# q and k of an attention kernel turned by VectorE in 32x32 blocks instead of by TensorE through PSUM

## Chip, cores and metric

The kernel runs on one core of a Trainium2 chip. The metric is the device time of one execution in microseconds (us). The core's engines are TensorE (PE; its weight loads are listed as PEld), VectorE (DVE), ScalarE (ACT), GpSimd (POOL) and SyncE (SP), which here only issues DMA transfers. Each engine works through its own instructions in order, and they wait for one another by semaphores.

## The reference, cut to what matters

An attention block whose scores are masked by a hash of q and k, followed by a Fourier mixing block with an MLP. Batch 4, 8 heads, 768 tokens, head dimension 64; everything is float32.

```python
q_bits = (einsum('bhsd,dk->bhsk', q, proj) > 0)          # 6 bits; the same for k
q_bucket = sum(q_bits * 2 ** arange(6), axis=-1)          # the same for k
mask = q_bucket[:, :, :, None] == k_bucket[:, :, None, :]
scores = where(mask, q @ k.T / sqrt(64), -1e9)
attn = softmax(scores)
x = (attn @ v), heads side by side                        # (4, 768, 512)

u = x + real(fft(fft(x, axis=1), axis=2))
un = layernorm(u)
out = u + relu(un @ w_ch1) @ w_ch2                        # 512 -> 2048 -> 512
```

## The kernel before

Two heads are handled together as a **pair**: 4 batches of 4 pairs, n = 0 to 15. The channels of both heads (2 x 64) fill the 128 partitions, so the scores need q and k with channels on partitions and tokens along the free dimension (`qt`, `kt`, 128 x 768), while DRAM holds tokens by rows of 64 channels. One tile with tokens on partitions is loaded per tensor:

```python
def load(n, names="qkv", second=nc.sync):
    b, t = divmod(n, NPAIR)
    for nm in names:
        src = {"q": q, "k": k, "v": v}[nm]
        tag, bufs = ("vn", 2) if nm == "v" else ("qkn", 2)
        tl = wt([P, NT, 2, D], F32, tag, f"{nm}n{n}", bufs)      # P=128, NT=6, D=64
        for h in range(2):
            (second if h else nc.sync).dma_start(
                tl[:, :, h, :], src[b, 2 * t + h].rearrange("(p c) d -> p c d", c=NT)
            )
        nat[nm, n] = tl
```

q and k share two buffers of the tag `qkn`: the q tile of a pair takes the buffer of the q tile of the pair before it, and k that of k.

`prepare(n)` turns the tiles by TensorE: six transposes of 128x128 for q and six for k, three in one PSUM bank, each bank copied to SBUF by VectorE or ScalarE in turn (`evac`). In the pairs of `LITE` after pair 0 all these copies go to ScalarE. Then come the sums of squares for a later check (`norm`) and the hash bits.

```python
def evac(dst, src, act=False):
    flip[0] ^= 1
    if flip[0] and not act:
        nc.vector.tensor_copy(dst, src)
    else:
        nc.scalar.copy(dst, src)

def prepare(n):
    lite = n in LITE                      # LITE = (0, 1, 2, 3, 4)
    act = lite and n > 0
    ts = {}
    for io, nm in enumerate("qk"):
        tn = nat.pop((nm, n))
        tt = wt([P, S], F32, nm + "t", f"{nm}t{n}")
        for g in range(2):
            ps = pt([P, 3, P], f"tr{nm}{n}_{g}")
            for i in range(3):
                c = 2 * i + g if nm == "q" else 3 * g + i
                nc.tensor.transpose(
                    ps[:, i, :], tn[:, c].rearrange("p h d -> p (h d)"), ident
                )
            if nm == "q":
                for i in range(2):
                    dst = tt[:, i * HALF + g * HALF // 2 : i * HALF + (g + 1) * HALF // 2]
                    evac(
                        dst.rearrange("p (j c) -> p c j", c=3),
                        ps[:, :, i * D : (i + 1) * D], act,
                    )
            else:
                evac(tt[:, g * HALF : (g + 1) * HALF],
                     ps.rearrange("p c t -> p (c t)"), act)
        ts[nm] = tt
        yield
        norm(n, io, tn)                   # ScalarE: squares of tn, summed by partition
    ...                                   # hash bits of q and k, from ts
```

q's tokens are stored with even tokens ahead of odd ones within each half, as the Fourier part needs them; k's order is free as long as v has the same.

The scores, their exponentials and the product with v run in six steps a pair; the next pair is prepared beside them, from the second step on:

```python
def attention(b):
    for t in range(NPAIR):
        n = NPAIR * b + t
        if 1 < n + 1 < NPAIR * B:
            load(n + 1)
        ahead = prepare(n + 1) if n + 1 < NPAIR * B else iter(())
        ...
        for c in range(NT):
            new = weigh(n, c)             # score products, Exp (ACT, L834), mask
            ...                           # sums of the weights (DVE, L913)
            while pending:
                finish()                  # product with v (L851)
            ...
            if c > 0:
                next(ahead, None)
            yield
```

PSUM has eight banks: two double banks `sc` for scores, two banks `o` for the product with v, and two banks `ps` for all the rest (`pt`), which are the transposes, the hash bits and every product of the MLP. The attention of batch 0 runs beside the conversion of the MLP's first weights, in the order of the program. The attention of batches 1 to 3 runs beside the Fourier part and the MLP of the batch before, in an order that the compiler's scheduler chose. The MLP uses fast (seven-product) matrix multiplication; its weight combinations are kept in DRAM and fetched by SyncE into a ring of twelve tiles (`w<-ad`), and into larger tiles (`w<-bd`).

At the end the largest norms of q and k decide whether a second, general kernel has to run in place of this one; for these inputs it doesn't:

```python
nc.vector.tensor_tensor(mt[:, 3:4], mt[:, 0:1], mt[:, 1:2], op=ALU.mult)
nc.vector.tensor_scalar(mt[:, 4:5], mt[:, 3:4], (SAFE / SCALE) ** 2, None, op0=ALU.is_gt)
```

Of the kernel before, what the change touches and what calls it, by code (L numbers as in the profile page):

```python
# [11 lines left out]
F32 = mybir.dt.float32  # L12
# [4 lines left out]
AF = mybir.ActivationFunctionType  # L17
ALU = mybir.AluOpType
AX = mybir.AxisListType

P = 128
B, H, S, D = 4, 8, 768, 64
# [3 lines left out]
NT = S // P  # L26
# [9 lines left out]
SCALE = 1.0 / float(np.sqrt(D))  # L36
# [7 lines left out]
SAFE = 36.0  # L44
# [435 lines left out]
def _main(  # L480
# [13 lines left out]
    nc = tc.nc  # L494
# [13 lines left out]
    def wt(shape, dtype, tag, name, bufs=2):  # L508
        return work.tile(shape, dtype, tag=tag, name=name, bufs=bufs)
# [12 lines left out]

    flip = [0]

    def evac(dst, src, act=False):

        flip[0] ^= 1
        if flip[0] and not act:
            nc.vector.tensor_copy(dst, src)
        else:  # L530
            nc.scalar.copy(dst, src)  # L531


    nat = {}

    def load(n, names="qkv", second=nc.sync):
        b, t = divmod(n, NPAIR)
        for nm in names:
            src = {"q": q, "k": k, "v": v}[nm]
            tag, bufs = ("vn", 2) if nm == "v" else ("qkn", 2)  # L540
            tl = wt([P, NT, 2, D], F32, tag, f"{nm}n{n}", bufs)
            for h in range(2):
                (second if h else nc.sync).dma_start(
                    tl[:, :, h, :], src[b, 2 * t + h].rearrange("(p c) d -> p c d", c=NT)
                )
            nat[nm, n] = tl

    load(0, "qk", nc.scalar)
    warm = const.tile([1, 1], F32, tag="warm", name="warm")
# [153 lines left out]
    def norm(n, io, tn):  # L703
        junk = wt([P, S], BF16, "junk", f"sq{io}_{n}", 1)
        nc.scalar.activation(
            junk, tn.rearrange("p c h d -> p (c h d)"), AF.Square,
            accum_out=norms[:, io, n : n + 1],
        )

    def prepare(n):  # L710

        lite = n in LITE
        act = lite and n > 0
        ts = {}
        for io, nm in enumerate("qk"):
            tn = nat.pop((nm, n))
            tt = wt([P, S], F32, nm + "t", f"{nm}t{n}")
            for g in range(2):  # L720
                ps = pt([P, 3, P], f"tr{nm}{n}_{g}")
                for i in range(3):
                    c = 2 * i + g if nm == "q" else 3 * g + i
                    nc.tensor.transpose(
                        ps[:, i, :], tn[:, c].rearrange("p h d -> p (h d)"), ident
                    )
                if nm == "q":
                    for i in range(2):
                        dst = tt[:, i * HALF + g * HALF // 2 : i * HALF + (g + 1) * HALF // 2]
                        evac(  # L730
                            dst.rearrange("p (j c) -> p c j", c=3),
                            ps[:, :, i * D : (i + 1) * D], act,
                        )
                else:
                    evac(
                        tt[:, g * HALF : (g + 1) * HALF],
                        ps.rearrange("p c t -> p (c t)"), act,
                    )
            ts[nm] = tt
            yield  # L740
            norm(n, io, tn)
        if lite:


            qk = wt([P, 2, S], BF16, "qb", f"qkb{n}")
            for io, nm in enumerate("qk"):
                for g in range(2):
                    cols = slice(g * HALF, (g + 1) * HALF)
                    ps = pt([P, HALF], f"bits{nm}{n}_{g}")
                    nc.tensor.matmul(ps, pjw, ts[nm][:, cols], start=True, stop=True)  # L750
                    bits = qk[:, io, cols]
                    nc.vector.tensor_scalar(
                        bits, ps, 0.0, off[:, io : io + 1],
                        op0=ALU.is_gt, op1=ALU.subtract,
                    )
                    if io == 0:
                        nc.vector.tensor_scalar(bits, bits, BIG, None, op0=ALU.mult)
                yield
            preps[n] = ts["q"], ts["k"], qk, None
            return  # L760

        ps = pt([P, HALF], f"bits{n}")
        for j in range(4):
            src = ts["qk"[j // 2]][:, (j % 2) * HALF : (j % 2 + 1) * HALF]
            nc.tensor.matmul(
                ps[32 * j : 32 * j + 32, :], pj, src, start=True, stop=True
            )
        bt = wt([P, HALF], BF16, "bt", f"bt{n}")
        nc.vector.tensor_scalar(bt, ps, 0.0, None, op0=ALU.is_gt)
        yield  # L770

        qb = wt([P, 2, S], BF16, "qb", f"qb{n}")
        kb = wt([P, 2, NT], F32, "kb", f"kb{n}")
        for h in range(2):
            ps = ps_sc.tile([P, 2, 512], F32, tag="sc", name=f"qb{n}_{h}")
            for g in range(2):
                rows = slice(32 * g, 32 * g + 32)
                with behind() if g + h else nullcontext():
                    last[0] = nc.tensor.matmul(
                        ps[:, g, 0:HALF], pw[rows, h, :], bt[rows, :],  # L780
                        start=True, stop=True,
                    )
            evac(qb[:, h, :].rearrange("p (g s) -> p g s", g=2), ps[:, :, 0:HALF])
        ps = ps_sc.tile([P, 2, 512], F32, tag="sc", name=f"kb{n}")
        for c in range(NT):
            g, i = divmod(c, NT // 2)
            rows = slice(64 + 32 * g, 96 + 32 * g)
            with behind() if c else nullcontext():
                last[0] = nc.tensor.matmul(
                    ps[:, g, 2 * i : 2 * i + 2], bt[rows, i * P : (i + 1) * P],  # L790
                    pw[rows, :, 0], start=True, stop=True,
                )
        nc.vector.tensor_copy(
            kb.rearrange("p h (g i) -> p g i h", g=2),
            ps[:, :, 0:NT].rearrange("p g (i h) -> p g i h", h=2),
        )
        preps[n] = ts["q"], ts["k"], qb, kb
# [48 lines left out]
    def values(n, c, pk, oos):  # L846

        for g in range(2):
            w = HALF + 1 - g
            for h in range(2):  # L850
                nc.tensor.matmul(  # L851
                    oos[g][h * D : (h + 1) * D, 0:w], nat["v", n][:, c, h, :],
                    pk[:, g, h, 0:w], start=(c == 0), stop=(c == NT - 1),
                )

# [229 lines left out]
    at = NR * 2 * P  # L1085
# [326 lines left out]
    for b in range(B):  # L1412
        if b > 0:

            wait = 0
            if b == 1:
                next(other)
                next(other)  # L1420
                wait = 2
            steps, done = NPAIR * NT - wait, 2 if b == 1 else 0
            for i, _ in enumerate(attention(b), 1):
                if b == 1 and i == 2:
                    for f, avg in means:
                        centre(f, avg)
                while done * steps < (MIX[b - 1] - LEFT) * (i - wait):
                    next(other)
                    done += 1
        if b == B - 1:  # L1430
            roomy[0] = True


            ms = const.tile([P, 3], F32, tag="ms", name="ms")
            nc.vector.tensor_reduce(ms[:, 0:2], norms, axis=AX.X, op=ALU.max)
            nc.vector.tensor_reduce(ms[:, 2:3], strange, axis=AX.X, op=ALU.max)
            ps = pt([1, 3, P], "norms_t")
            for io in range(3):
                nc.tensor.transpose(ps[:, io, :], ms[:, io : io + 1], ident)
            mt = const.tile([1, 5], F32, tag="mt", name="mt")  # L1440
            nc.vector.tensor_reduce(mt[:, 0:3], ps, axis=AX.X, op=ALU.max)
            nc.vector.tensor_tensor(mt[:, 3:4], mt[:, 0:1], mt[:, 1:2], op=ALU.mult)
            nc.vector.tensor_scalar(
                mt[:, 4:5], mt[:, 3:4], (SAFE / SCALE) ** 2, None, op0=ALU.is_gt
            )
            fl = const.tile([1, 1], I32, tag="fl", name="fl")
            nc.vector.scalar_tensor_tensor(
                fl, mt[:, 2:3], 0.0, mt[:, 4:5], op0=ALU.is_gt, op1=ALU.max
            )
            large = nc.values_load(fl[0:1, 0:1], min_val=0, max_val=1)  # L1450
        for _ in other:
            pass
        other = mix(b)
        if b == 0:
            arrival2 = weights2()
            other = after(2 + NT, other, islice(arrival2, HF + 1))
# [47 lines left out]
```

## Time and profile before

The median of three executions is 1155.78 us (1155.18 to 1157.42). The profiled execution has a span of 1153.1 us.

| what | where it is read | value |
|---|---|---|
| granted TensorE clock, mean | list of cores | 0.995 |
| instructions | head of the page | 14159 |
| DMA packets | slices | 126414, of which 81408 under 512 B |
| bytes moved | slices | 103.13 MB, mean 89 GB/s |
| load of one q or k tile | DMA issues | two transfers of 192 KB, 3.4 and 3.5 us to landing |
| ring load `w<-ad` | DMA issues | 128 KB, 2.0 us to landing, 168 of them |
| one exponential `pk<-sc` (L834) | groups | 808 ns on ACT, 192 of them |

A line of a group names the source line, the engine, the operation, the tile written and those read, and the shape; behind the count come the busy time of the group in us and the mean of one in ns, and then the idle time of the engine just ahead of these instructions, with what ended it. L529 and L531 are the two copies inside `evac`, so they stand for all its callers; the tile names tell them apart. L724 is the transpose. Busy times of matmuls overlap, as TensorE pipelines them, and idle time of an engine that bounds nothing costs nothing.

### The profile page before, as it was taken

The page shows a single profiled execution, that of the slowest core. Times are in us where ns is not written, and L with a number is a line of the kernel's source. Part 1 is how long each engine was busy: PE and PEld are TensorE (multiplying, and loading weights), DVE is VectorE, ACT ScalarE, POOL GpSimd, SP SyncE. Part 2 cuts the span into 40 slices and gives each one's busy share as a digit, 9 for nine tenths or more (in the row PEclk, how much of TensorE's full clock was granted, in tenths as well). Part 3 has the DMA queues.
Part 4 walks back from the last instruction along what each step waited for, and adds up shares of the span by engine and source line. Part 5 has one row for each costly group of instructions (what it writes and reads, how often), then busy time and mean ns, then how long its engine had stood idle before and what let it go on. Part 6 is the DMA issues. An engine that isn't in the chain of part 4 may idle for free. (4 is left out here: it accounts for less than half of the span.)

```text
span 1153.1 us, 14159 instructions
## 1 busy us (share of the span) xinstructions
PE 1092.3 (95%) x5065; PEld 669.3 (58%) x5065; DVE 803.5 (70%) x1445; ACT 464.8 (40%) x892; POOL 81.3 (7%) x157
## 2 busy tenths in 40 slices
PE   7989888899998999999999999999999999999996
PEld 4444344454754576644674467654575468768675
DVE  4889968728689487884867777885775877644352
ACT  6778345524155223345224531345424431341420
POOL 1000000002100011020000002002000002000002
PEclk9999999999999999999999999999999999999998
DMA  9524144600126115013042315013114214131401
GB/s 271 153 79 122 39 138 141 217 16 19 28 83 228 51 51 192 14 51 105 19 151 65 88 51 179 14 42 96 46 34 135 65 31 170 43 92 61 142 19 39
DMA packets 126414, 103.13 MB, mean 89 GB/s; under 512 B 81408, under 2 KB 113280, under 8 KB 126336
## 3 DMA queue, kind: packets, MB, share of 16 engines
q1 hardware_dynamic: 118608, 82.35, 24.3%
q0 software_dynamic: 6160, 19.40, 5.2%
q8 instruction: 42, 0.69, 0.2%
q10 hardware_dynamic: 1568, 0.39, 0.2%
q14 instruction: 36, 0.29, 0.1%
HBM read 81.14 MB, written 20.97 MB: 89 GB/s over the span
## 5 line engine op out<-in xcount | busy, mean ns | idle before, releaser
L1188 PE MATMUL o<-w,h 128*128 128x256 f32 x1152 | 259.5, 381 | 0.3
L1188 PEld LDWEIGHTS o<-w,h 128*128 128x128 f32 x1152 | 216.1, 190 | 41.0 <-issue 4.9
L834 ACT ACTIVATE pk<-sc 128x768 f32<-128x768 f32 x192 | 147.9, 808 | 89.9 <-PE sc L830 63.7
L840 DVE SCALAR_TENSOR_TENSOR pk<-qb,kb,pk 128x768 f32<-128x768 bf16 x132 | 129.5, 1013 | 53.7 <-ACT pk L834 53.6
L851 PE MATMUL oo<-pk,vn 128*64 128x385 f32 (+1 forms) x768 | 149.8, 498 | 5.1 <-ACT x L863 3.6
L830 PE MATMUL sc<-qt,kt 64*128 64x384 f32 x768 | 152.7, 501 | 1.1 <-ACT pk L834 1.1
L1317 PE MATMUL h_p<-x,w 128*128 128x384 f32 x384 | 140.2, 494 | 2.1 <-ACT qt L531 0.6
L913 DVE TENSOR_TENSOR acc<-acc,pk 128x1536 f32<-128x1536 f32 (+1 forms) x80 | 113.3, 1433 | 9.2 <-ACT pk L834 8.4
L1317 PE MATMUL h_p<-w 128*128 128x384 f32 x288 | 106.3, 492 | 2.9 <-ACT qt L531 1.7
L851 PEld LDWEIGHTS oo<-pk,vn 128*64 128x64 f32 x768 | 48.0, 136 | 94.7 <-issue 69.8
L1317 PEld LDWEIGHTS h_p<-x,w 128*128 128x128 f32 x384 | 69.7, 190 | 56.5 <-ACT h L1349 3.4
L1270 PE MATMUL h<-x,w 128*128 128x384 f32 x256 | 88.5, 498 | 5.3 <-ACT kt L531 2.7
L830 PEld LDWEIGHTS sc<-qt,kt 64*128 64x128 f32 x768 | 66.8, 186 | 43.8 <-issue 22.6
L1317 PEld LDWEIGHTS h_p<-w 128*128 128x128 f32 x288 | 53.1, 190 | 43.4 <-ACT qt L531 2.4
L1270 PEld LDWEIGHTS h<-x,w 128*128 128x128 f32 x256 | 48.1, 193 | 41.1 <-ACT h L1274 3.5
L941 POOL DMA_DIRECT2D out_dram<-w x40 | 21.9, 548 | 555.3 <-issue 426.5
L1200 DVE SCALAR_TENSOR_TENSOR w<-o,rs,w 128x256 f32<-128x256 f32 x56 | 26.9, 481 | 46.0 <-PE o L1188 45.7
L1218 ACT COPY tq<-o 128x256 f32<-128x256 f32 x24 | 8.9, 371 | 109.5 <-PE o L1188 109.5
L1188 PE MATMUL o<-w 128*128 128x256 f32 x192 | 46.3, 384 | 2.8 <-DVE u L1200 1.9
L1188 PEld LDWEIGHTS o<-w 128*128 128x128 f32 x192 | 35.7, 190 | 11.1 <-DVE w L1200 2.7
L1003 PE MATMUL cs<-ch,z 128*128 128x128 f32 (+3 forms) x192 | 31.8, 316 | 6.4 <-ACT kt L531 2.6
L1207 ACT COPY tq<-o 128x256 f32<-128x256 f32 x24 | 8.9, 370 | 66.9 <-PE o L1188 66.9
(155 smaller groups left out, 1320.9 us busy)
## 6 DMA issues: line engine op xcount, KB each, us to landing
w<-ad SPq DMA_DIRECT2D x168, 128.0 KB, 2.0
w<-bd SPq DMA_DIRECT2D x42, 512.0 KB, 4.5
zraw<-in_moe_w_ch_dram POOLq DMA_DIRECT2D x21, 512.0 KB, 4.2
bd<-w SPq DMA_DIRECT2D x14, 512.0 KB, 4.5
vn<-in_v_dram SPq DMA_DIRECT2D x32, 192.0 KB, 3.3
qn<-in_q_dram SPq DMA_DIRECT2D x31, 192.0 KB, 3.4
kn<-in_k_dram SPq DMA_DIRECT2D x31, 192.0 KB, 3.5
ad<-tq SPq DMA_DIRECT2D x8, 512.0 KB, 3.4
```

What stands on the lines that cost most here:

```text
L830: last[0] = nc.tensor.matmul(ps[:, h, 0:HALF], kt[rows, ks], qt[rows, qs], start=kb is not None, stop=True,)
L834: nc.scalar.activation(pk[:, g, :, 0:HALF], ps[:, :, 0:HALF], AF.Exp, scale=SCALE)
L840: nc.vector.scalar_tensor_tensor(w, qb[:, h].rearrange("p (g s) -> p g s", g=2), kb[:, h, c : c + 1], w, op0=ALU.is_equal, op1=ALU.mult,)
L851: nc.tensor.matmul(oos[g][h * D : (h + 1) * D, 0:w], nat["v", n][:, c, h, :], pk[:, g, h, 0:w], start=(c == 0), stop=(c == NT - 1),)
L913: nc.vector.tensor_tensor(acc[:, g], (first if c == 1 else acc)[:, g], new[:, g, :, 0:HALF], op=ALU.add,)
L941: nc.gpsimd.dma_start(out[b, s0 : s0 + 2 * w - 1 : 2, cols], src[at : at + w, cols])
L1003: nc.tensor.matmul(ps[:, pc + 2 * lo : pc + 2 * hi - 1 : 2], z[:, cp, pc, par, t * P : (t + 1) * P], ch[:, cp, pc, lo:hi], start=(cp == 0) ...
L1188: nc.tensor.matmul(ps, a[:, r], right7[i][:, r], start=start and r == 0, stop=r == HF // 2 - 1, skip_group_check=not start,)
L1200: nc.vector.scalar_tensor_tensor(t[:, cols], src, r, t[:, cols], op0=ALU.mult, op1=ALU.add)
L1207: nc.scalar.copy(qq, p1)
L1270: nc.tensor.matmul(ps, w1[:, c, fc * P : (fc + 1) * P], x[:, c, cols], start=(c == 0), stop=(c == NDC - 1),)
L1317: nc.tensor.matmul(ps, ring[n % NR][:, k], right[i][:, k], start=start and k == 0, stop=k == 1, skip_group_check=not start,)
```

## The change

For all pairs but the first, q and k are loaded so that 32x32 blocks of them can be turned in place by VectorE. A tile's 128 partitions are four groups of 32. Group i takes one channel quarter of the pair (head i // 2, channels 32 * (i % 2) and on); within it, partition p holds token p of each block of 32 tokens, and the 24 blocks with 32 channels each lie along the free dimension. One VectorE transpose of the whole 128 x 768 tile turns each block, so that channels lie on partitions and tokens along the free dimension. For q the loads take even and odd tokens apart, so that the parity order comes from the load and from the order in which the transpose walks the tile. TensorE and PSUM have no part in it any more. The rows that a transfer reads and writes are 128 bytes, where they were 256, and there are four transfers for k and eight for q in place of two.

Three things follow from it. v of all pairs, and k of pair 0, are loaded with token c * 128 + p at partition p, slot c, to match k's new order, still in 256-byte rows. Pair 0 is turned by TensorE as before. The sums of squares are now over a quarter of the channels each, and the threshold is lowered by a factor of four to be on the safe side. `evac` loses its argument `act`, as only pair 0 still copies transposes.

The diff, cut to its core:

```diff
-    def evac(dst, src, act=False):
+    def evac(dst, src):
         flip[0] ^= 1
-        if flip[0] and not act:
+        if flip[0]:
...
-            tl = wt([P, NT, 2, D], F32, tag, f"{nm}n{n}", bufs)
-            for h in range(2):
-                (second if h else nc.sync).dma_start(
-                    tl[:, :, h, :], src[b, 2 * t + h].rearrange("(p c) d -> p c d", c=NT)
-                )
+            tl = wt([P, S], F32, tag, f"{nm}n{n}", bufs)
             nat[nm, n] = tl
+            if nm == "v" or n == 0:
+                tc_ = tl.rearrange("p (c h d) -> p c h d", c=NT, h=2)
+                for h in range(2):
+                    s = src[b, 2 * t + h]
+                    s = (
+                        s.rearrange("(p c) d -> p c d", c=NT) if nm == "q"
+                        else s.rearrange("(c p) d -> p c d", p=P)
+                    )
+                    (second if h else nc.sync).dma_start(tc_[:, :, h, :], s)
+                continue
+            for i in range(4):
+                s = src[b, 2 * t + i // 2, :, i % 2 * 32 : i % 2 * 32 + 32]
+                d = tl[32 * i : 32 * i + 32]
+                if nm == "k":
+                    nc.sync.dma_start(
+                        d.rearrange("p (j a) -> p j a", a=32),
+                        s.rearrange("(j b) a -> b j a", b=32),
+                    )
+                else:
+                    s = s.rearrange("(j b r) a -> r b j a", b=32, r=2)
+                    d = d.rearrange("p (r j a) -> r p j a", r=2, a=32)
+                    for r in range(2):
+                        nc.sync.dma_start(d[r], s[r])
...
         lite = n in LITE
-        act = lite and n > 0
         ts = {}
         for io, nm in enumerate("qk"):
             tn = nat.pop((nm, n))
             tt = wt([P, S], F32, nm + "t", f"{nm}t{n}")
-            for g in range(2):
+            if n > 0:
+                to, at = tt, tn
+                if nm == "q":
+                    to = tt.rearrange("p (i r n) -> p r i n", i=2, r=2)
+                    at = tn.rearrange("p (r i n) -> p r i n", i=2, r=2)
+                nc.vector.transpose(to, at)
+            for g in range(2) if n == 0 else ():
                 ps = pt([P, 3, P], f"tr{nm}{n}_{g}")
                 ...                       # transposes and copies as before, without act
...
-                mt[:, 4:5], mt[:, 3:4], (SAFE / SCALE) ** 2, None, op0=ALU.is_gt
+                mt[:, 4:5], mt[:, 3:4], (SAFE / SCALE / 2) ** 2, None, op0=ALU.is_gt
```

More of the change, by code (lines that the diff above doesn't have):

```diff
@@ L705, in norm @@
         nc.scalar.activation(
-            junk, tn.rearrange("p c h d -> p (c h d)"), AF.Square,
+            junk, tn, AF.Square,
             accum_out=norms[:, io, n : n + 1],
@@ L723, in prepare @@
                     c = 2 * i + g if nm == "q" else 3 * g + i
-                    nc.tensor.transpose(
-                        ps[:, i, :], tn[:, c].rearrange("p h d -> p (h d)"), ident
-                    )
+                    nc.tensor.transpose(ps[:, i, :], tn[:, c * P : (c + 1) * P], ident)
                 if nm == "q":
@@ L731, in prepare @@
                             dst.rearrange("p (j c) -> p c j", c=3),
-                            ps[:, :, i * D : (i + 1) * D], act,
+                            ps[:, :, i * D : (i + 1) * D],
                         )
@@ L736, in prepare @@
                         tt[:, g * HALF : (g + 1) * HALF],
-                        ps.rearrange("p c t -> p (c t)"), act,
+                        ps.rearrange("p c t -> p (c t)"),
                     )
@@ L851, in values @@
                 nc.tensor.matmul(
-                    oos[g][h * D : (h + 1) * D, 0:w], nat["v", n][:, c, h, :],
+                    oos[g][h * D : (h + 1) * D, 0:w], nat["v", n][:, (2 * c + h) * D : (2 * c + h + 1) * D],
                     pk[:, g, h, 0:w], start=(c == 0), stop=(c == NT - 1),
```

## The prediction, made before the changed kernel ran

> **What bounds the kernel now.** I read the page from the top: busy time per engine, then the 40 slices, then the groups at the transposes, then the waits of each engine, and last the timeline around single pairs. The chain that ended last holds only one queue entry of the last store, so it doesn't help here; the bound has to be read stage by stage.
>
> ```profile
> PE 1092.3 (95%) x5065; PEld 669.3 (58%) x5065; DVE 803.5 (70%) x1445; ACT 464.8 (40%) x892; POOL 81.3 (7%) x157
> ...
> PE   7989888899998999999999999999999999999996
> ...
> DVE  4889968728689487884867777885775877644352
> ...
> DMA  9524144600126115013042315013114214131401
> ```
>
> TensorE is busy 1092.3 of 1153.1 us and only 61 us idle, nearly everywhere at a nine. VectorE is dense only in the first five slices or so, which is attention of batch 0, where it also converts the weights. The DMA row is full in the first slice alone. A query by stages makes that exact:
>
> ```profile
> 0.00:155.00 155.00, 136.05 (x730) 62.96 (x732) 126.90 (x235) 102.79 (x189) 6.42 (x26) 1.00 0.50 139
> 155.00:960.00 805.00, 774.92 (x3568) 466.47 (x3565) 584.17 (x1022) 311.00 (x587) 55.58 (x92) 1.00 0.27 82
> ```
>
> After the window and its length the columns are PE, PEld, DVE, ACT and POOL busy (with instruction counts), the granted clock, the DMA share and GB/s. From 155 to 960 us, PE is busy 96% and DVE 73%: PE bounds. In the first 155 us PE has 88% and DVE 82%, and the timeline shows DVE working without a gap from 70 to 110 us: there the two are bound together, in program order.
>
> The groups of the transposes that the change removes, and of the two DVE transposes of the softmax sums, which are a sample of the instruction that it adds:
>
> ```profile
> L883 DVE STREAM_TRANSPOSE rb<-rt 128x384 f32<-128x384 f32 x32 | 18.4, 576 | 0.8
> L874 DVE STREAM_TRANSPOSE rt<-sum 128x384 f32<-128x384 f32 x32 | 18.4, 576 | 0.0
> ...
> L724 PE MATMUL trq<-ident,qn 128*128 128x128 f32 x96 | 16.3, 293 | 7.5 <-DMA qn<-in_q_dram 5.0 <-ACT qt L531 1.8 <-DVE u L1200 0.4
> ...
> L724 PE MATMUL trk<-ident,kn 128*128 128x128 f32 x96 | 15.8, 289 | 2.4 <-ACT qt L531 1.4 <-DVE F L1016 0.7 <-DMA kn<-in_k_dram 0.3
> ...
> L531 ACT COPY qt<-trq 128x192 f32<-128x192 f32 x40 | 14.8, 431 | 36.7 <-DVE qt L529 36.7
> ...
> L529 DVE COPY qt<-trq 128x192 f32<-128x192 f32 x24 | 9.7, 410 | 9.1 <-PE trq L724 8.8
> ...
> L529 DVE COPY kt<-trk 128x384 f32<-128x384 f32 x12 | 6.6, 552 | 3.5 <-PE trk L724 3.5
> ```
>
> The reader is to see that the mean of 290 ns is a latency, not a cost: 96 of them are busy for 16.3 us together, because they overlap. The timeline gives the spacing:
>
> ```profile
> 109.20 0.87 PE L724 MATMUL trk<-ident,kn 128*128 128x128 f32 x6
> ...
> 304.15 0.49 PE L724 MATMUL trk<-ident,kn 128*128 128x128 f32 x3
> ```
>
> Six end after 0.87 us, three after 0.49 us; with 0.27 us for the first, each further one adds 0.11 to 0.12 us.
>
> **What the Trainium skill says.** "TensorE: Matmul & The Clock Gate", Part 4 (PE-mode transpose), gives about 275 ns for a 128x128 transpose in a kernel's context; the trace's fastest are 272 ns, so it agrees as a latency. "Vector Engine (DVE) Microarchitecture Reference", 3.8, says that the 32x32 transpose sustains one element per cycle and lane; with the 0.96 GHz of "VectorE: DVE Perf Modes" (Specifications) 384 elements would take 400 ns, and the trace's 576 ns is that plus a fixed 176 ns. "DMA: Bandwidth & Descriptors" says, under "Why small descriptors are slow (HBM only)", that a packet carries a fixed overhead beside its bytes, so halving the packets to 128 B doesn't halve their time. The trace before has only the larger packets for q and k, so this is not yet shown.
>
> **The change, part by part.**
>
> TensorE loses 12 transposes in each of 15 pairs, 180 in all. At 0.11 to 0.12 us each that is about 21 us, of which 132 (pairs 5 to 15, the first of them at 142 us) come after batch 0's attention: 132 x 0.115 = 15 us on the engine that bounds. The other 48 (pairs 1 to 4) are 5.5 us within the mixed stage.
>
> Waits around them go too. In the steady part only two PSUM buffers serve all of this, so a slow copy out holds TensorE. TensorE's own waits there whose releaser is a qt or kt copy, or that stand ahead of a transpose, are (the same view): h on kt 2.7, cs on kt 2.6, h_p on qt 2.3, transposes on qt 1.8 and 1.4, h on qt 1.0, transposes on other buffers 1.1; 13 us together. Some of these would have become another wait, as the next product waits for its own copy; I choose half, 6 us.
>
> VectorE gains 30 transposes of 128x768. From 384 elements at 576 ns and a slope of 400 ns for 384 more (tensor operations of 384 and 768 elements show 555 and 952 ns, the same slope) each takes about 0.98 us: 29 us. It loses its share of the copies: in pairs 5 to 15 two of four q copies and one of two k copies, 22 x 0.41 + 11 x 0.55 = 15 us. In pairs 1 to 4 all copies were ScalarE's, so VectorE loses nothing there and gains 8 x 0.98 = 7.8 us. ScalarE loses 38 x 0.43 + 19 x 0.48 = 25 us, of which 10.7 us lie in pairs 1 to 4. So from 155 us on VectorE gets 22 - 15 = 7 us more at 73% load, off the path. In batch 0 it gets 7.8 us more at 82%, partly on the path.
>
> For batch 0 I look at what stands behind a transpose of pair 3 or 4. From the six at 109.20 us it takes 2.1 us to the next score product, of which 1.2 are a wait for an exponential:
>
> ```profile
> 111.30 0.34 PE L823 MATMUL sc<-qkb 64*128 64x384 bf16 x2 [1.22 <-ACT pk L834]
> ```
>
> The exponentials themselves run beside four or two copies on the in-order ScalarE. Taking transposes and copies away frees some 2 us a pair on PE and 2.7 us on ACT, while DVE gets 2 us a pair more. Where DVE has gaps (pairs 1 and 2) I expect 1 to 1.5 us won a pair, where it has none (70 to 110 us) a like loss. Net: 0, give or take 4 us.
>
> DMA: a q or k tensor is 1536 packets of 256 B in two transfers now and 3072 packets of 128 B in four (k) or eight (q) after. One q load alone, with no other traffic around it, reads:
>
> ```profile
> 296.00:297.00 1.00, 0.89 (x4) 0.68 (x4) 0.48 (x1) 0.22 (x1) 0.00 (x0) 1.00 0.19 45
> 297.00:298.00 1.00, 1.00 (x6) 0.87 (x6) 0.00 (x0) 0.00 (x0) 0.00 (x0) 1.00 0.99 226
> 298.00:299.00 1.00, 1.00 (x7) 0.87 (x6) 0.00 (x0) 0.37 (x1) 0.00 (x0) 1.00 0.51 115
> ```
>
> Shares of 0.19, 0.99, 0.51 and 0.04 in the slice after sum to 1.73 us of sixteen engines: 18 ns for a packet on an engine. If a 128 B packet takes between half of that and all of it, a tensor takes 1.7 to 3.5 us of DMA time, 0 to 3.5 us more a pair, at a DMA share of 0.27: hidden. The SyncE queue issues twelve instead of four; the present ones take 0.55 to 0.6 us each for 768 packets, and a ring load of 128 KB 0.33 us, so 4 x 0.55 + 8 x 0.35 to 0.55 gives 5 to 6.6 us instead of 2.4 us a pair. The loads are issued as soon as the last tile was read (q of the next pair at 295.36 us, just behind its predecessor's transposes) and used tens of us later, so landing later costs nothing from batch 1 on. The ring loads queued behind wait 3 to 4 us more; the ring is twelve deep, and a product uses about 0.65 us of TensorE, so 8 us are covered.
>
> At the start it is different: DMA is at 0.8 to 1.0 in the first 30 us, the load of pair 1 is issued at 8.9 us, and its transposes begin at 17.5 us. Its 0 to 3.5 us more and the same again for pair 2 push the weights behind it. I put 2 us on the path for that.
>
> Sum: -15 (transposes) - 6 (waits) + 0 (batch 0) + 2 (start) = -19 us, rounded to 1155.8 - 19.8 = **1136 us**.
>
> **Rivals.**
>
> First, VectorE becomes the bound of batch 0. For it speaks DVE's gapless stretch from 70 to 110 us and that the old kernel kept its copies off VectorE in pairs 1 to 4. Against it: gaps of 3 to 6 us at 64 to 68 and 110 to 122 us. Then the 7.8 us come in full and only 12 to 14 us stay: 1143 us.
>
> Second, the loads starve something: SyncE is in order, and a load that waits for its tile holds up ring loads behind it; with twelve entries and small packets, products could wait for weights. Against it: TensorE shows no wait for the ring of 0.3 us or more now. If it came, 1 us a pair would make 1148 us.
>
> Third, the PSUM buffers were worth more than I counted. All 13 us of waits go and the batch 0 stage wins its 2 us a pair as well: 15 + 5 + 13 + 5 gives 1118 to 1122 us. For it speaks that TensorE is the bound in 70% of the span, with two buffers.
>
> Fourth, the order of batches 1 to 3 isn't the program's: instructions are placed by a scheduler's model, so a removal reshuffles what runs beside what. That is good for some 5 us either way.
>
> **Range and chances.** The PE term of 15 us is firm; waits, batch 0 and the start carry about 4 to 6 us each. That gives 1120 to 1153 us for 8 in 10. A gain of over 2% needs less than 1132.7 us, 3 us beyond my centre, so 0.38; slower by over 2% would take a starved ring or start of 40 us: 0.04; the rest, 0.58, is within 2%.
>
> **What would show it.** PE busy should fall by some 20 us, with 5065 - 180 = 4885 matmuls, and its idle time from 61 us to about 55. STREAM_TRANSPOSE groups of 128x768 with 0.95 to 1.0 us, 30 of them; a mean far above that breaks the DVE step. The first 155 us stage should end within 4 us of before; if score products there wait more for pk and DVE has no gap, the first rival holds. New PE waits at the bits products on DVE's qt or kt would be the wait that takes the old one's place. Waits for DMA at qt, kt or the weights in the first 40 us above 3 us in sum break the start step; PE waits at the ring products for DMA break the ring step.

## The result, and the profile after

The changed kernel takes 1129.51 us (median of four, 1127.22 to 1131.2), against 1156.6 us for the kernel before in the same comparison: a ratio of 0.9766, 95% interval 0.9744 to 0.9787. The profiled span went from 1153.1 to 1125.4 us. The page after, again the busy times and then the rows of 40 slices:

```profile
PE 1067.8 (95%) x4885; PEld 652.0 (58%) x4885; DVE 813.7 (72%) x1442; ACT 445.8 (40%) x835; POOL 81.3 (7%) x157
...
PE   7988887999999999999999999999999999999995
...
DVE  5889987927689596984777797995966876644352
...
DMA  9643525442037234212244225023023214122301
```

TensorE has lost its 180 transposes and 24.5 us of busy time; its idle time fell from 61 to 57.6 us. It still stands at a nine from the eighth slice on; the first seven, mostly sevens and eights, are batch 0 and the step into batch 1. The new VectorE instructions, as groups (count, then busy us and mean ns):

```profile
L747 DVE STREAM_TRANSPOSE qt<-qn 128x768 f32<-128x768 f32 x15 | 14.6, 973 | 6.7 <-PE sc L856 6.5
L747 DVE STREAM_TRANSPOSE kt<-kn 128x768 f32<-128x768 f32 x15 | 14.5, 968 | 0.0
```

Thirty at 0.97 us, as estimated. The 6.5 us behind the bar are a wait for the buffer of `qt`, still read by score products; VectorE had room for it. The DMA part of the page:

```profile
DMA packets 174415, 103.13 MB, mean 92 GB/s; under 512 B 129408, under 2 KB 161280, under 8 KB 174336
...
q1 hardware_dynamic: 166608, 82.35, 27.6%
...
qn<-in_q_dram SPq DMA_DIRECT2D x120, 48.0 KB, 2.4
kn<-in_k_dram SPq DMA_DIRECT2D x60, 96.0 KB, 3.2
```

48000 packets more for the same bytes.

The most telling view is not a line of the page. In each pair one short product, the sum of the weights (`sum<-acc`), runs once all its steps are done, so its start marks the end of the pair. From the timelines, one execution of each kernel, in us from the span's start, with the end of TensorE's work:

| kernel | pair 0 | pair 1 | pair 3 | pair 4 | pair 5 | pair 9 | pair 15 | end |
|---|---|---|---|---|---|---|---|---|
| before | 42.4 | 73.9 | 128.6 | 188.9 | 264.7 | 557.8 | 950.0 | 1141.7 |
| after | 41.4 | 74.5 | 130.2 | 188.7 | 262.8 | 543.0 | 922.3 | 1114.0 |
| late_only | 42.3 | 73.8 | 127.8 | 181.5 | 256.7 | 537.6 | 917.0 | 1108.8 |
| early_only | 41.3 | 74.5 | 130.2 | 191.2 | 267.2 | 560.3 | 952.5 | 1144.3 |
| pe_unread | 43.2 | 76.3 | 132.0 | 186.2 | 264.2 | 549.9 | 935.0 | 1126.8 |
| pe_column | 41.1 | 74.3 | 130.0 | 185.4 | 266.8 | 556.3 | 947.9 | 1139.6 |
| dve_twice | 43.8 | 79.5 | 139.2 | 198.5 | 275.2 | 556.1 | 936.4 | 1128.1 |
| wide_loads | 40.9 | 74.1 | 129.7 | 187.7 | 262.9 | 542.7 | 923.3 | 1115.0 |
| fetch_on_sync | 42.8 | 76.0 | 131.6 | 186.3 | 260.9 | 540.8 | 920.1 | 1111.9 |
| late_one | 41.7 | 73.2 | 127.3 | 182.4 | 257.9 | 538.8 | 918.1 | 1109.9 |
| late_sync | 42.3 | 73.8 | 127.7 | 180.6 | 256.1 | 536.6 | 915.9 | 1107.7 |

Read the second row against the first: batch 0 (pairs 0 to 3) loses 1.6 us, pair 4 makes that good, and all of the gain comes between the ends of pairs 4 and 15, some 2.5 us a pair. The last stretch, where nothing is prepared any more, is the same in both.

How far can such differences be trusted? The end of pair 0 scatters: it lies between 41.3 and 42.8 us in after, early_only and fetch_on_sync, which are the same program up to there. From the end of pair 0 to that of pair 3, the kernel before takes 86.2 us, and every kernel with one VectorE transpose per tile in pairs 1 to 4 takes 88.8 or 88.9: the loss in batch 0 is 2.6 us. From the end of pair 5 to that of pair 15, before and early_only take 685.3 us, and after, late_only, wide_loads and fetch_on_sync 659.2 to 660.4. Pairs 4 and 5 scatter far more between kernels of like work.

Where it comes from within TensorE's time can be summed up from the timeline: for each product, the time from the start of a row to the start of the next, from pair 4's end on.

| us of TensorE's time on | before | after | pe_unread | pe_column |
|---|---|---|---|---|
| `trq`, `trk` (transposes) | 18.6 | 0 | 18.6 | 22.1 |
| `h`, `h_p` (MLP, first half) | 323.7 | 315.4 | 314.7 | 315.3 |
| `bits` | 10.5 | 7.8 | 7.8 | 10.5 |
| `sc`, `oo` (scores, product with v) | 199.0 | 199.0 | 200.8 | 205.3 |

So 18.6 of the 27.5 us are the transposes themselves, with the waits right at them. The other 9 lie at other products, most of them (8.3) at `h` and `h_p`, which have nothing to do with q and k but use the same PSUM banks or the same engines for their copies; `bits` gives 2.7 more, and small losses elsewhere take 2 back.

### The profile page after: what moved, and what is told of

It reads as the page before. It is cut to its first block, busy times and chain, and to the rows that moved or that the text cites. A ratio compares the mean times of both kernels' runs of the same rounds, so it can differ in the third digit from the quotient of the medians.

```text
span 1125.4 us, 13920 instructions
## 1 busy us (share of the span) xinstructions
PE 1067.8 (95%) x4885; PEld 652.0 (58%) x4885; DVE 813.7 (72%) x1442; ACT 445.8 (40%) x835; POOL 81.3 (7%) x157
## 3 DMA queue, kind: packets, MB, share of 16 engines
q1 hardware_dynamic: 166608, 82.35, 27.6%
## 5 line engine op out<-in xcount | busy, mean ns | idle before, releaser
L1214 PEld LDWEIGHTS o<-w,h 128*128 128x128 f32 x1152 | 216.7, 190 | 41.7 <-issue 2.3
L967 POOL DMA_DIRECT2D out_dram<-w x40 | 21.9, 550 | 538.8 <-issue 412.7
L1214 PEld LDWEIGHTS o<-w 128*128 128x128 f32 x192 | 35.7, 190 | 12.3 <-DVE w L1226 3.9
L1300 ACT ACTIVATE h<-h 128x384 f32<-128x384 f32 x32 | 15.6, 489 | 48.7 <-PE h L1296 48.5
```

Source lines behind the costliest of these rows:

```text
L967: nc.gpsimd.dma_start(out[b, s0 : s0 + 2 * w - 1 : 2, cols], src[at : at + w, cols])
L1214: nc.tensor.matmul(ps, a[:, r], right7[i][:, r], start=start and r == 0, stop=r == HF // 2 - 1, skip_group_check=not start,)
L1300: nc.scalar.activation(hall[:, i, r, cols], ps, AF.Relu)
```

## The experiments

**late_only and early_only: one part of the pairs alone.** late_only has VectorE's way for pairs 5 to 15 only, early_only for pairs 1 to 4 only (in `load` and, with the old copies, in `prepare`):

```diff
-            if nm == "v" or n == 0:
+            if nm == "v" or n <= 4:                  # late_only
+            if nm == "v" or (n == 0 or n > 4):       # early_only
```

> Only pairs 5 to 15 are turned by VectorE; pairs 1 to 4 go back to TensorE with their copies on ScalarE. Theory A (the gain lies wholly after batch 0, and batch 0 pays 1.6 us for 7.8 us of added VectorE work): 1127 to 1129 us, 1 to 2 us below the changed kernel, and the pair ends of batch 0 as in the kernel before. Rival (batch 0's loss is the price of something it gives back later, or is noise of the order): equal to the changed kernel within 0.5 us or slower.

> Only pairs 1 to 4 are turned by VectorE, pairs 5 to 15 as before. Theory A: 1 to 2 us slower than the kernel before (1157 to 1159 us). Rival (the early part gains 2 us a pair on TensorE and ScalarE, as my third rival had it): 1148 to 1152 us. If early_only and late_only add up to the full change (sum of both differences near -27 us), the two parts are independent.

late_only took 1121.39 us, ratio 0.969 (0.9669 to 0.9711), clear of the full change and faster than it by 8 us, where I had expected 1 to 2. early_only took 1161.32 us, ratio 1.0044 (1.0026 to 1.0063): slower than before by 3 to 7 us, more than the 1 to 2 I had expected (its row in the table, a single execution, ends 2.6 us later). The part in batch 0 costs, then, and the later part carries more than the whole gain. The two differences add up to about -31 us, 4 us more than the full change shows; so something in the full change costs extra. The table says where: late_only needs 53.7 us from the end of pair 3 to that of pair 4, the full change 58.5, the kernel before 60.3. So the step into batch 1 could have gained 6.6 us and gained 1.8.

**pe_unread and pe_column: TensorE's share taken apart.** pe_unread puts the transposes back, into the same banks, with nobody reading them. pe_column has one column of each bank read as well.

```diff
                 nc.vector.transpose(to, at)
+                for g in range(2):
+                    ps = pt([P, 3, P], f"tr{nm}{n}_{g}")
+                    for i in range(3):
+                        c = 2 * i + g if nm == "q" else 3 * g + i
+                        nc.tensor.transpose(ps[:, i, :], tn[:, c * P : (c + 1) * P], ident)
+                    col = wt([P, 1], F32, "col", f"col{nm}{n}_{g}", 4)     # from here
+                    if g or n in LITE:                                     # on only
+                        nc.scalar.copy(col, ps[:, 2, P - 1 : P])           # in
+                    else:                                                  # pe_column
+                        nc.vector.tensor_copy(col, ps[:, 2, P - 1 : P])
```

> The changed kernel with the 180 transposes by TensorE put back into the same PSUM banks, but nobody reads them; q and k still come from VectorE. Theory A (the gain is two halves: TensorE's own time, and banks held until a copy comes): only the first half comes back, 15 to 20 us, so 1144 to 1150 us. Rival B (all of it is TensorE's time, with gaps around each group): 1154 to 1157 us, the time of before. Rival C (TensorE's time is absorbed in gaps): under 1138 us.

> As pe_unread, but one column of each bank is copied out by VectorE or ScalarE in turn (ScalarE in pairs 1 to 4), so that a bank is held until the copying engine gets there, at almost no cost to that engine. Theory A (held banks are the second half): 6 to 13 us above pe_unread, 1152 to 1160 us. Rival D (the rest was the copies' own time on VectorE and ScalarE): within 3 us of pe_unread.

pe_unread took 1138.54 us (0.9836, 0.9811 to 0.986): 9 us above the full change by the medians, 12.8 by the spans of the profiles, which show the slowest of its executions and the fastest of the full change. That is less than the 15 to 20 us of theory A and barely above the 1138 of rival C. Part of the miss is pair 4, which pe_unread passes in 54.2 us, without what held up the full change there. From pair 4 to the end the full change gains 27.5 us on the kernel before, pe_unread 12.3, so 15.2 come back. Over the steadier stretch from the end of pair 5 to that of pair 15, with 108 transposes, 11.3 of 25.8 us come back.

pe_column took 1152.34 us (0.9958, 0.9946 to 0.997), 14 us above pe_unread and still a little below the kernel before. From pair 5 to pair 15 it takes back another 10.3 us, and 4.2 of the 25.8 stay gained. Counted from pair 4 on it takes back 13.7 and nothing stays (-1.4), but that count has pair 5's own stretch in it, where TensorE's granted clock fell in pe_column (0.50 from 193 to 196 us). The columns are next to no work: ACT's busy time is 449.0 us against 444.9 in pe_unread.

So of the 25.8 us, 11.3 are TensorE's own time and 10.3 come from having to be read by another engine, however little. The last 4.2 stay open: the kernel before has six wider copies a pair where pe_column has four columns, and its engines' order differs a little. By place the two don't match either. In pe_column `h` and `h_p` stay at 315.3 us, where the kernel before has 323.7, and the time comes back at the transposes, at `sc` and `oo`, `bits` and the last product of the MLP. That being read costs this much is shown, then; that the waits of the kernel before were these same ones is not. TensorE's waits in pe_column between 186 and 950 us (total us, times, longest) show little of it by the columns' name:

```profile
PE trk L752 <- ACT h L1310: 2.3, 1, 2.3
...
PE h_p L1353 <- ACT colk L755: 0.7, 2, 0.4
PE trk L752 <- DVE colk L757: 0.7, 3, 0.3
PE cs L1039 <- DVE colk L757: 0.7, 2, 0.3
```

The coupling has two sides that these runs don't separate: a bank is held until the in-order reader gets to it, and the reader, once there, waits for TensorE with its other copies behind it.

The order of the instructions changed too, if little. Without the transposes and their copies, 4611 of TensorE's 4873 matmuls stand in the same order before and after, 1303 of 1409 instructions of VectorE and 740 of 832 of ScalarE. Between pe_unread and pe_column it is 4731, 1381 and 813. So order can hardly explain what the columns cost, but it may have a share in the whole gain, which no run here measures.

**dve_twice: VectorE's share.** Each transpose is issued twice.

```diff
                 nc.vector.transpose(to, at)
+                nc.vector.transpose(to, at)
```

> The changed kernel with each of the 30 VectorE transposes done twice into the same tile: 29 us more VectorE work, 7.8 us of it in pairs 1 to 4. Theory A (VectorE has room after batch 0 and little within it): from pair 4 on the gain is kept within 3 us, batch 0's attention ends 3 to 6 us later than in the changed kernel; in all 4 to 8 us slower, 1133 to 1138 us. First rival in full (VectorE bounds): 20 us or more slower.

1141.0 us (0.984, 0.9822 to 0.9859), 11.5 us slower than the full change and more than I expected, in both stages. The doubled transposes add 7.8 us in batch 0, and its end moves by 9.0 us (139.2 against 130.2); from the end of pair 0 to that of pair 3 they add 5.8 us and cost 6.6. There VectorE is the bound. After it, 21 us more of VectorE move the end by 5 us, 1.7 of them from pair 5 to pair 15. VectorE's waits between 40 and 130 us, in the kernel before and then in the full change, and last the stretch in the full change (columns as in the prediction; DVE is the third time):

```profile
DVE w L638 <- PE wm L630: 5.0, 2, 3.3
DVE acc L913 <- ACT pk L834: 2.2, 3, 1.2
```

```profile
DVE w L662 <- PE wm L654: 3.3, 1, 3.3
```

```profile
40.00:130.00 90.00, 74.77 (x414) 31.04 (x412) 82.89 (x150) 58.54 (x100) 2.75 (x6) 1.00 0.44 98
```

One wait of 3.3 us in 90 us, and 82.9 us busy: an engine that hardly ever waits for another. In the kernel before this stretch had 80.69 us of DVE and 81.61 of PE; now PE has only 74.77 and waits. The kernel before still had three waits of VectorE for exponentials (`acc` on `pk`), 2.2 us together; the new transposes fill them.

**wide_loads: the small rows.** q and k come in two transfers of 256-byte rows again; VectorE turns what lies there, blocks of mixed tokens and channels, so the output isn't the reference's, with the same work everywhere else.

```diff
-            if nm == "v" or n == 0:
+            if True:
                 tc_ = tl.rearrange("p (c h d) -> p c h d", c=NT, h=2)
...
-            for i in range(4):
-                ...                        # the loads of channel quarters
```

> The changed kernel, but q and k of all pairs are loaded as before in two transfers of 256-byte rows; VectorE then turns blocks that mix other tokens and channels, so the output is not the reference's, with the same instructions on TensorE, VectorE and ScalarE. It tells what the small rows cost. Theory A (the loads are hidden except at the start): 0 to 2 us faster, 1127.5 to 1130 us, with the difference in the first 40 us. Rival (small rows and twelve issues hold up other transfers): 4 us or more faster, spread over the pairs.

1128.04 us (0.9731, 0.9713 to 0.9748): 1.5 us below the full change by the medians. By the ratios it is 4 us, and the two intervals just touch, so the times alone leave a cost of a few us open; but the pair ends agree within 1 us, and no stretch shows one. The queue's line gives an estimate of their price on the DMA engines:

```profile
q1 hardware_dynamic: 118608, 82.35, 25.2%
```

27.6% less 25.2% of sixteen engines over 1125 us are 432 us for the 30 tensors, which had 46080 packets at 18 ns, 829 us, before. So 92160 packets took 1261 us: about 14 ns for 128 bytes against 18 for 256, so halving a packet doesn't halve its time. It makes 1.8 us more a pair, hidden.

**fetch_on_sync: what held up pair 4.** In the full change's trace VectorE stands idle from 168.3 to 174.8 us. VectorE, then TensorE:

```profile
167.29 1.01 DVE L1042 COPY F<-cs 128x510 f32<-128x510 f32 x2
174.78 0.42 DVE L1131 TENSOR_TENSOR tq<-w 128x256 f32<-128x256 f32 x1 [6.48 <-DMA ad<-tq]
175.12 0.42 DVE L1133 TENSOR_TENSOR tq<-w 128x256 f32<-128x256 f32 x1
175.45 1.01 DVE L1074 TENSOR_TENSOR x<-x,A 128x384 f32<-128x384 f32 x2
```

```profile
170.09 0.81 PE L1058 MATMUL B<-sq,F 128*128 128x192 f32 x4
...
176.61 1.28 PE L1058 MATMUL A<-sq,F 128*128 128x193 f32 x4 [3.35 <-DVE x L1074]
177.68 1.49 PE L1058 MATMUL B<-sq,F 128*128 128x193 f32 x4
178.97 1.48 PE L1058 MATMUL A<-sq,F 128*128 128x192 f32 x4
180.25 0.89 PE L1058 MATMUL B<-sq,F 128*128 128x192 f32 x4
```

A combination of MLP weights (`tq`) is stored to DRAM, and the next one is written into the same tile. The store went out at 167.4 us, just behind these fetches by GpSimd:

```profile
166.22 1.57 POOL L677 DMA_DIRECT2D zraw<-in_moe_w_ch_dram  x3 [54.52 <-ACT F L1036]
...
167.40 0.37 SPq L1137 DMA_DIRECT2D ad<-tq  x1
```

The fetches are three of 512 KB each, and the store shares the DMA engines with them (DMA share 0.85 to 1.01 in stretches of 2 us from 168 to 174). VectorE, in order, holds back the additions at L1074 that free the banks of `A` and `B`, and TensorE runs dry. In late_only, as before the change, the fourth combination of this stretch is begun some microseconds earlier, behind a store that meets no fetches, and the next comes much later. The edit queues the fetches behind the store:

```diff
             for i in range(arrival.depth) if half == 0 else ():
-                arrival.fetch(i, nc.gpsimd)
+                arrival.fetch(i, nc.sync)
```

> The changed kernel with the first three fetches of the second weights issued by SyncE, behind the store of the last weight combination, instead of by GpSimd ahead of it. The changed kernel's trace has VectorE waiting 6.5 us for this store at 168 to 175 us, with TensorE idle for 3.4 us and its clock lowered behind it, while the kernel with TensorE's transposes in pairs 1 to 4 has no such wait. If the store's collision with the three fetches is why that stretch gained nothing: 3 to 6 us faster, 1124 to 1127 us, with the wait gone. If the wait only stands for another one: no change.

1126.81 us (0.9724, 0.9709 to 0.9739), 2.7 us below the full change. Pair 4 took 54.7 us instead of 58.5, nearly late_only's 53.7. VectorE's wait for the store from 128 to 192 us:

```profile
DVE tq L1131 <- DMA ad<-tq: 4.9, 2, 2.6
```

Two of together 4.9 us, where the full change has 9.2, and TensorE's wait for L1074 in that product is gone. So the collision is the cause of 3.8 us in that stretch, in this order of instructions. It isn't the only thing that can hold up pair 4: wide_loads has no more than 2.5 us of these waits and took 58.0 us there, with TensorE waiting 2.0 and 2.6 us for other engines instead.

**late_one and late_sync: a better version?** late_one is late_only with pair 1 turned by VectorE too (`n == 0 or 2 <= n <= 4` for the old way); late_sync is late_only with the edit of fetch_on_sync.

> As late_only (1121.4 us), but pair 1 too is turned by VectorE; pairs 2 to 4 stay with TensorE. In the changed kernel the first pair ended 1.0 us earlier than before and only the pairs behind it lost. If the loss begins with pair 2: 0.5 to 1.5 us faster than late_only, 1120 us. If the small rows at the start cost the pair behind it: equal or 1 us slower.

> late_only (1121.4 us) together with the edit of fetch_on_sync. In late_only VectorE had only 0.6 us of waits for the store, so if that wait was what fetch_on_sync removed, the two don't add: 1120 to 1123 us. If issuing the fetches by SyncE is worth something by itself: 1118 to 1119 us.

late_one took 1122.23 us (0.969, 0.9664 to 0.9717), late_sync 1121.06 us (0.9672, 0.9645 to 0.9699). Neither differs from late_only by more than the runs scatter. That late_sync gains nothing fits: late_only had only 0.6 us of that wait. late_one leaves open whether pair 1 is worth its 1 us; from the end of pair 0 to that of pair 3 it takes 85.6 us, late_only 85.5. The better version is late_only, 8 us below the full change.

## Why the prediction was right, step by step

It said 1136 us within 1120 to 1153; 1129.5 lies inside, and the gain was 27 us instead of 20. (The terms of its sum add up to 19, not 19.8.) That the miss is no larger is in part luck: the waits gave 6 to 8.5 us more than I had put in, no loss shows at the start, and a collision that I hadn't foreseen took 4 us back. Its steps:

- **Transposes, 15 us:** right. Put back unread, they took 15.2 us from pair 4 on (120 of them) or 11.3 from pair 5 on (108), 0.10 to 0.13 us each, where I had 0.115.
- **Waits around them, 6 of 13 us:** this is the term that was mis-sized. Beside the transposes' own time the change gains 27.5 - 15.2 = 12.3 us from pair 4 on, or 25.8 - 11.3 = 14.5 from pair 5 on, twice what I took; pe_column takes back 13.7 or 10.3 of them. In size the third rival was right here. My reason for taking half, that another wait would follow in their place, didn't hold. But the 13 us that I had counted aren't what went: they were from the whole run, and 4.0 of them (`cs` on `kt`, `trk` on `qt`) lie in the stretch of pair 4. TensorE's waits for q and k copies in the kernel before between 189 and 950 us make 7.8 us,

```profile
PE h L1270 <- ACT kt L531: 2.7, 1, 2.7
...
PE h_p L1317 <- ACT qt L531: 2.3, 3, 1.7
...
PE trq L724 <- ACT qt L531: 1.8, 2, 0.9
...
PE h L1270 <- ACT qt L531: 1.0, 1, 1.0
```

and after, no wait at `h_p` or `h` is longer than 1.1 us. More went than carries a name in that list; most of it is spread thin.

- **Batch 0, 0 give or take 4, and the start, 2 us lost:** right in sum, 1.6 us lost by the end of pair 3, and wrong in place. No loss shows at the start: the end of pair 0 lies within its scatter, and wide loads changed little. What was lost, 2.6 us from the end of pair 0 to that of pair 3, was VectorE's. Six of its transposes, 5.8 us, fall there. Some 2 us of them filled its waits for exponentials, and most of the rest came in full, as the doubled ones did; there the first rival's mechanism is the true one. I had expected 1 to 1.5 us a pair from the relief of TensorE and ScalarE in pairs 1 and 2; TensorE's part of it gave nothing: pe_unread, with the transposes back on TensorE, takes the same 88.8 us. What ScalarE's relief gave, no run shows alone.
- **VectorE off the path after batch 0:** nearly right; 21 us more cost 5 us, so the net 7 us of the change may have cost 1 or 2 (an estimate).
- **Loads hidden, ring not starved:** right. 14 ns a packet lies in the middle of the range I took, and no wait of a ring product for DMA is in TensorE's list.
- **The scheduler's order, 5 us either way:** the order of TensorE changed little, but a few us of this kind came from a transfer that now met other transfers. I had looked for such a collision at the loads; it was at a store, and 3.8 us of the possible gain went there.

## What to carry to other kernels

An operation on TensorE that must be read out of PSUM can cost more than its own time. Here, where two banks served many products, being read by another in-order engine cost about as much again, even when the copy was one column wide; moving the operation to an engine that works from SBUF to SBUF removed both. Ask stage by stage whether the receiving engine has room: here the same move gained 2.5 us a pair where VectorE was 73% busy, and lost where VectorE hardly ever waited. Move it only in the stages that gain.

## What was not expected of the hardware

After TensorE's dry spell before 176.6 us (3.35 us of idle time in its records) its granted clock fell. Three stretches of 1 us of the full change, with the clock behind the busy times of PE, PEld, DVE, ACT and POOL:

```profile
176.00:177.00 1.00, 0.39 (x2) 0.42 (x3) 1.00 (x3) 0.00 (x0) 0.00 (x0) 0.99 0.00 0
177.00:178.00 1.00, 1.00 (x5) 0.87 (x4) 1.00 (x4) 0.00 (x0) 0.00 (x0) 0.50 0.00 0
...
180.00:181.00 1.00, 1.00 (x6) 0.84 (x4) 1.00 (x4) 0.27 (x2) 0.00 (x0) 0.81 0.00 0
```

Three groups of four products took 1.28, 1.49 and 1.48 us, where the same ones a little earlier took 0.81 to 0.92. The clock records have 3.4 us at 0.50 there, so a wait of 3.4 us cost about 1.7 us more behind it (an estimate: half of 3.4). It wasn't the only one: the next long gap of the same trace, 3.0 us before 193.5 us, was followed by another 3.4 us at 0.50.
